# A store of one output piece, dealt in four transfers instead of one

## The chip, the cores and the metric

The kernel runs on one core of one Trainium2 chip. Its time is device microseconds from one launch to its end; the time before is the median of six runs. One execution was also taken by the hardware profiler; the profile and the trace below are of that execution.

## The reference

Cross-covariance attention over four quarters (batch entries) of 6400 rows and 256 columns, followed by a mixture of eight low-rank adapters on every row, two of the eight chosen by a gate. Only the shape of the output matters for the change: 25,600 rows of 256 fp32 numbers, 26.2 MB.

```python
qn = q / (norm(q, axis=1) + 1e-6); kn = k / (norm(k, axis=1) + 1e-6)
a = softmax(kn.T @ qn / tau)            # 256 x 256 for each quarter
x = (v @ a).reshape(25600, 256)
logits = x @ w_gate; w = softmax of the two largest of eight
out = x + sum over the chosen e of w_e * ((x @ A[e]) @ B[e])
```

## The kernel before, in words

A quarter's 6400 rows are laid on 128 partitions, 50 rows ("chunks") to a partition, so that partition p holds rows 50p to 50p+49 of the quarter. The q and k rows of a quarter come in three loads each, and its v rows in five loads of ten chunks. A piece (b, i) is quarter b, ten chunks from 10i. For each quarter the kernel accumulates k'q and the norms (`do_G`, L636), makes the softmax matrix, and then, for each of the five pieces, transposes v (`do_T`, L822), computes the gate and the adapters, and multiplies (`do_Y`, L949). `do_Ye` (L963) copies a pair of chunks of the result from PSUM into the piece's slot of the tile `Y` in SBUF (seven slots of ten chunks; `STORE`, L250), and `do_store` (L966) sends the piece to the output in HBM.

The order of the work on every engine is written out ahead of time: `make_plan` (L276) lists the steps with their costs and what they wait for, `Plan.run` (L105) plays the list through against a model of the engines, the buffers and the transfers, and the instructions are issued in the order that results. The planner sees a store as one step on SP (L434); it does not look at `SPLIT` or `SHARES`. The order of the steps, the slots and the banks are therefore the same before and after the change.

There are three places where transfers are issued. Loads go out from GpSimd (`do_load`, L613, L627; queue q0 in the profile, converting fp32 to bf16 on the way). Stores go out from SP in the order of the plan (L971; queue q1). The first q and k chunks and the weights go out from SP and ScalarE at the start. A store carries for every partition ten chunks of one piece, a run of 10,240 bytes in SBUF and in HBM, so a store of 128 partitions has 128 rows of 10,240 bytes. The last two pieces of the last quarter go in stores of 4, 4 and 2 chunks (`FINE`, L461, L432), which have shorter rows.

`HOLD` (L456) makes some stores wait for a load that has nothing to do with their data. Piece (2, 3) is in it, and waits for the load of v (0, 4), which landed long before; its wait ends at once.

The SP order from the changed store on is: (2, 3), (2, 4), (3, 0), (0, 1), (3, 1), (3, 2), three parts of (3, 3), three parts of (3, 4). Of the slots that these stores free, only that of (2, 3) is filled again, by the copies of piece (3, 4).

The lines of `do_store` that the change reaches:

```python
        for rows in SHARES if (b, i) in SPLIT else (P,):
            r = nc.sync.dma_start(out_v[b, p:p + rows, lo:lo + n, :], Y[p:p + rows, at_y:at_y + n, :])
...
            p += rows
```

Of the kernel before, what the change touches and what calls it, by code (L numbers as in the profile page):

```python
# [458 lines left out]

PARTS = {(0, 0): ((0, 4), (4, 13)), (0, 2): ((34, 8), (42, 8)), (3, 2): ((34, 8), (42, 8))}  # L460
FINE = 2  # L461
SPLIT, SHARES = set(), ()
OFF = {(0, 0, 'k'), (0, 1, 'q'), (0, 2, 'q'), (0, 3, 'q'), (0, 5, 'q'), (0, 6, 'k'), (0, 8, 'k'), (1, 0,
        'k'), (1, 1, 'k'), (1, 2, 'k'), (1, 2, 'q'), (1, 3, 'q'), (1, 4, 'k'), (1, 5, 'q'), (1, 6, 'k'), (1,
        6, 'q'), (2, 0, 'k'), (2, 0, 'q'), (2, 3, 'q'), (2, 5, 'k'), (2, 5, 'q'), (2, 6, 'k'), (2, 7, 'q'),
# [569 lines left out]
```

## Time and profile before

| what | value |
|---|---|
| median of six runs | 254.53 us (254.22 to 254.84) |
| the profiled execution: its time, its span | 254.84 us, 253.1 us |
| TensorE matmul busy | 222.7 us, 88% of the span |
| VectorE, ScalarE busy | 170.9 us (68%), 158.1 us (62%) |
| loads (q0), stores and first loads (q1) | 38.80 MB, 26.87 MB |
| instruction fetches (q8) | 19 packets, 0.31 MB |
| mean granted clock of TensorE | 0.958 |

The span runs from the first instruction to the last; the time of an execution also holds what lies around it, 1.7 us here. The profile's section 2 cuts the span in 40 slices and gives for each the busy share of every engine in tenths, the mean busy share of the 16 DMA engines, and the rate at which they moved bytes. Section 3 counts what each DMA queue moved. Section 4 is the chain of work that ended last. A DMA engine's part of a transfer is called a ring here. A transfer's landing is told to a semaphore in 16 steps; the trace keeps the time of each step, and the start, length and size of every packet that a ring moved.

### The profile page before, as it was taken

How to read it: one execution, taken by the hardware profiler on the slowest of the kernel's cores; microseconds unless marked ns; L12 is line 12 of the kernel's file. 1: busy time of each engine (PE TensorE's matmuls, PEld its weight loads, DVE VectorE, ACT ScalarE, POOL GpSimd, SP SyncE). 2: the span in 40 equal slices, each digit the busy share in tenths (PEclk: the TensorE clock that was granted, in tenths of full speed). 3: DMA queues.
4: the chain of work that ended last, by engine and by line, in shares of the span. 5: the costliest groups of instructions: out<-in, count | busy, mean ns of one | idle time of the engine just before them, and what ended most of it. 6: DMA issues, size and time to landing. Idle time of an engine off the chain costs nothing.

```text
span 253.1 us, 6005 instructions
## 1 busy us (share of the span) xinstructions
PE 222.7 (88%) x2467; PEld 197.6 (78%) x2467; DVE 170.9 (68%) x485; ACT 158.1 (62%) x294; POOL 26.6 (11%) x54
## 2 busy tenths in 40 slices
PE   0677996799999899999998998899999999999960
PEld 0465884599899898889996997699978889999940
DVE  0024374469997988786849679869996897597420
ACT  5424123276877758767665778756954948877840
POOL 7003010011000201000102203010000200000000
PEclk9959997599999999999999999999999999999996
DMA  8999999999999999999999999999999999999994
GB/s 249 216 217 210 212 221 212 214 220 214 218 211 224 308 216 221 308 292 239 220 214 302 232 217 213 210 214 215 213 312 411 418 230 322 334 403 427 422 414 180
DMA packets 11147, 66.71 MB, mean 264 GB/s; under 512 B 1264, under 2 KB 1648, under 8 KB 6512
## 3 DMA queue, kind: packets, MB, share of 16 engines
q0 software_dynamic: 6912, 38.80, 74.3%
q1 hardware_dynamic: 3872, 26.87, 25.9%
q10 hardware_dynamic: 336, 0.66, 0.8%
q8 instruction: 19, 0.31, 0.4%
q14 instruction: 8, 0.07, 0.1%
HBM read 78.91 MB, written 26.21 MB: 415 GB/s over the span
## 4 chain that ended last, share of the span: by engine, by line
PE 56%; DMA 26%; DVE 9%; ACT 4%; issue 1%; POOL 0%; POOLq 0%; DVEq 0%
PE Y_ps L955 14%; DMA qk<-in_k_dram 14%; PE acc L642 9%; PE Y_ps L960 7%; DMA v<-in_v_dram 7%; PE T_ps L828 5%; DMA out_dram<-y 5%; PE gzT_ps L942 4%; PE Z_ps L919 4%; DVE ssq L670 4%; PE ZL_ps L852 3%; PE acc L646 3%; ACT sq L664 2%; PE acc L651 2%; PE log_ps L866 2%
## 5 line engine op out<-in xcount | busy, mean ns | idle before, releaser
L642 PE MATMUL acc<-qk 128*128 128x256 bf16 x400 | 75.6, 287 | 13.2 <-ACT qk L815 6.6
L670 DVE TENSOR_TENSOR ssq<-ssq,sq 128x1280 f32<-128x1280 f32 (+1 forms) x27 | 43.3, 1604 | 25.8 <-ACT sq L664 25.5
L955 PE MATMUL Y_ps<-a_bf,vT 128*128 128x256 bf16 x400 | 60.0, 272 | 0.3 <-ACT y L810 0.3
L810 ACT COPY y<-Y_ps 128x512 f32<-128x512 f32 x83 | 47.9, 588 | 18.0 <-PE Y_ps L960 12.0
L664 ACT ACTIVATE sq<-qk 128x1280 f32<-128x1280 bf16 (+1 forms) x27 | 36.9, 1368 | 27.9 <-DMA qk<-in_k_dram 10.1
L642 PEld LDWEIGHTS <-qk 128*128 128x128 bf16 x400 | 36.1, 104 | 18.4 <-DMA qk<-in_k_dram 8.6
L955 PEld LDWEIGHTS <-vT 128*128 128x128 bf16 x400 | 38.7, 98 | 4.7 <-issue 0.5
L960 PE MATMUL Y_ps<-ball,gzT 128*128 128x256 bf16 x200 | 38.2, 273 | 0.0
L646 PE MATMUL acc<-qk 128*128 128x128 bf16 x210 | 30.2, 226 | 0.0
L651 PE MATMUL acc<-qk 128*128 128x128 bf16 x200 | 29.3, 231 | 0.0
L828 PE MATMUL T_ps<-ident,v 128*128 128x128 f32 x200 | 28.1, 274 | 0.0
L930 DVE TENSOR_TENSOR gz<-Z_ps,gateg 128x256 bf16<-128x256 f32 x60 | 22.4, 440 | 4.3 <-PE Z_ps L919 4.2
L810 ACT COPY vT<-T_ps 128x512 f32<-128x512 f32 (+1 forms) x43 | 21.7, 540 | 5.2 <-PE T_ps L828 4.9
L646 PEld LDWEIGHTS <-qk 128*128 128x128 bf16 x210 | 21.3, 101 | 3.1
L828 PEld LDWEIGHTS T_ps<-ident,v 128*128 128x128 f32 x200 | 22.1, 142 | 0.6 <-issue 0.2
L810 ACT COPY gzT<-gzT_ps 128x256 f32<-128x256 f32 (+1 forms) x45 | 14.7, 348 | 12.3 <-PE gzT_ps L942 12.2
L960 PEld LDWEIGHTS <-gzT 128*128 128x128 bf16 x200 | 19.4, 98 | 2.5 <-DVE gzT L812 0.3
L627 POOL DMA_DIRECT2D v<-in_v_dram x20 | 11.0, 551 | 98.5 <-PE T_ps L828 75.9
L651 PEld LDWEIGHTS <-qk 128*128 128x128 bf16 x200 | 19.1, 104 | 2.6
L942 PE MATMUL gzT_ps<-ident,gz 128*128 128x128 f32 x100 | 19.7, 281 | 1.4 <-DVE gz L930 1.0
L919 PE MATMUL Z_ps<-waA_sb,vT 128*128 128x128 bf16 x240 | 17.7, 219 | 0.0
L664 ACT ACTIVATE ssq<-qk 128x1536 f32<-128x1536 bf16 x8 | 11.9, 1485 | 7.1 <-DMA qk<-in_q_dram 3.6
(80 smaller groups left out, 275.4 us busy)
## 6 DMA issues: line engine op xcount, KB each, us to landing
out_dram<-y SPq DMA_DIRECT2D x18, 1280.0 KB, 12.6
v<-in_v_dram POOLq DMA_DIRECT2D x20, 640.0 KB, 25.2
qk<-in_q_dram POOLq DMA_DIRECT2D x7, 1088.0 KB, 22.6
qk<-in_k_dram POOLq DMA_DIRECT2D x7, 1088.0 KB, 27.1
qk<-in_q_dram POOLq DMA_DIRECT2D x4, 512.0 KB, 23.2
qk<-in_k_dram POOLq DMA_DIRECT2D x4, 512.0 KB, 24.8
qk<-in_q_dram POOLq DMA_DIRECT2D x2, 1024.0 KB, 30.5
qk<-in_k_dram POOLq DMA_DIRECT2D x2, 1024.0 KB, 35.0
```

What stands on the lines that cost most here:

```text
L642: nc.tensor.matmul(acc[ic][:, 0:256], kt[:, j, ic::CC], qt[:, j, :], start=c == 0, stop=False, skip_group_check=True)
L646: nc.tensor.matmul(acc[ic][:, 256:384], kt[:, j, ic::CC], kt[:, j, ic::CC], start=False, stop=False, skip_group_check=True)
L651: nc.tensor.matmul(acc[ic][:, 384:512], qt[:, j, ic * P:(ic + 1) * P], qt[:, j, ic * P:(ic + 1) * P], start=False, stop=c == NC - 1, skip_ ...
L664: nc.scalar.activation(out[:, 0:n, :], t[:, j:j + n, :], ACT.Square)
L670: nc.vector.tensor_tensor(out=t, in0=t, in1=held["sq", (w, b, g), ""][:, 0:n, :], op=OP.add)
L810: nc.scalar.copy(out, in_)
L828: nc.tensor.matmul(ps[:, j, :], vt[:, c + j, :].bitcast(FP32), W["ident32"], is_transpose=True, start=(j == 0), stop=(j == n - 1))
L919: nc.tensor.matmul(ps[:, j, :], vT_of(b, i, c + j)[:, :, ic], st[b]["aA"][:, ic, :], start=(j == 0 and ic == 0), stop=(j == n - 1 and ic = ...
L930: nc.vector.tensor_tensor(out=pairs[:, h].rearrange("p c (e r) -> p c e r", e=E), in0=z[:, 2 * h:2 * h + 2, :].rearrange("p c (e r) -> p c ...
L942: nc.tensor.matmul(ps[:, j, :], pairs[:, j * P:(j + 1) * P], W["ident32"], is_transpose=True, start=(j == 0), stop=(j == n // 2 - 1))
L955: nc.tensor.matmul(ps[:, j, :], vT_of(b, i, c + j)[:, :, ic], st[b]["a"][:, ic, :], start=(j == 0 and ic == 0), stop=False, skip_group_che ...
L960: nc.tensor.matmul(ps[:, j, :], pair[:, :, j], W["B"], start=False, stop=(j == 1), skip_group_check=True)
```

## The change

The store of piece (2, 3), the 128 rows of 10,240 bytes that are the partitions 0 to 127, goes out in four transfers of 112, 6, 6 and 4 rows (partitions 0 to 111, 112 to 117, 118 to 123 and 124 to 127), issued one after the other from SP. Only the first of them carries the `HOLD` dependency. The bytes, their source and their place in the output stay as they are.

```diff
-SPLIT, SHARES = set(), ()
+SPLIT, SHARES = {(2, 3)}, (112, 6, 6, 4)
```

## The prediction

> **What bounds the kernel now.** The change touches one store, issued at 211.61 us of a span of 253.1, so I read from the end backwards: first what ends last, then what that waits for, then whether the transfers before it have slack.
>
> The waits of SP from 244 us to the end (who waited for whom: us in total, times, longest):
>
> ```profile
> SPq L1030 <- DMA out_dram<-y: 6.4, 5, 2.8
> SPq L971 <- ACT y L810: 1.6, 2, 1.4
> ```
>
> L1030 is the end of the program. SP waits there for stores to land, five times, 6.4 us together. The compute engines are done long before: the chain of work from 244 us on ends with
>
> ```profile
> 244.32 0.59 ACT y L810
> ```
>
> (start, length), a copy that ends at 244.91, and the last store is issued at 244.93. The last step of its landing comes at 252.15 in the trace's landing records; the span ends 0.9 us later. So stores set the end. Is it their latency or their bytes? The DMA view of 226 to 253 us, in 40 slices of 0.68 us:
>
> ```profile
> DMA  9999999999999999999999999999999986631100
> GB/s 419 425 410 425 425 437 425 425 425 425 455 410 410 425 455 404 425 410 425 440 410 425 428 391 446 410 385 413 428 404 416 410 352 264 258 149 73 49 6 0
> ...
> q1 hardware_dynamic: 1664, 9.82, 87.4%
> q8 instruction: 2, 0.03, 0.4%
> ```
>
> It is bytes: the rings are 9 tenths busy or more for 32 slices, at some 425 GB/s, and then the rate falls in steps. That tail is the place of this change: some rings finish while others still work. The packets say how far apart. From 226 us each ring's packets follow one another without a gap until its last store packet, which ends at 247.6 to 248.4 us on six rings, at 249.7 to 250.3 on seven, and at 251.31, 251.34 and 251.82 on three. A store row of 10,240 bytes is one packet, and starts 381 ns after the one before it on its ring (409 on one ring of the seven). In every transfer of 128 rows each ring carries eight, so a lead or a lag once got is kept to the end. One cause of the lags is seen: an instruction fetch of 16 KB (19 of them, q8) takes 0.9 to 1.0 us of one ring, and those at 216.3 and 236.5 us hit two of the three late rings.
>
> So the end is the latest ring's: 251.82 us of packets, 0.33 to the landing step, 0.9 to close, and 1.7 around the span, 254.84 in all. That execution is 0.31 above the median of 254.53; I work in differences and put them on the median.
>
> **The change, part by part.** *SP.* Three more issues. An issue took 332 ns, up to 914 when another had just gone before, with 0.03 to 0.06 us for a wait ahead of it; three take 1.1 to 2.9 us, and SP is free at 215.2 at the latest. The next store is issued at 217.73, so this is hidden. If that cover went, the rings would still cover it: the earliest ring reaches that store's rows around 226.4. Stores take eight semaphores in turn; three more move each later store three on. One then finds its semaphore's earlier store still landing: (0, 1), issued at 224.11, would take that of the store that landed at 224.49. It goes 0.4 us late, SP has nothing behind it until 231.70, and its first rows move at about 232. Nothing.
>
> *Who waits for the store itself.* Its slot is filled again by piece (3, 4), whose first copy is this one:
>
> ```profile
> 241.22 1.24 ACT L810 COPY y<-Y_ps 128x512 f32<-128x512 f32 x2 [0.96 <-PE Y_ps L960]
> ```
>
> The store now lands at 230.59, so it may land 10 us later. The load of v (3, 4), issued at 212.35 beside it, has landed by 224.09, about when the earliest ring starts on (2, 3), and PE transposes it from 228.2. Hidden.
>
> *Fewer rows on most rings.* The 112 rows are seven a ring instead of eight. A transfer of six rows can use six rings at most. If the three small ones begin at the same ring, four rings get 7+3=10 rows, two get 9 and ten get 7: +0.76, +0.38 and -0.38 us. As all rings work without a gap to the end, that is carried to the end. If the six are early rings, they end at 249.2 or before, and the end is 251.82 - 0.38: a gain of 0.38 us. If the latest ring is one of the four, it costs 0.76. The trace does not number the rings. What it shows, as far as the landings can be followed, is that the instruction fetches go from ring to ring in turn: each later fetch makes another ring late. The rings hit longest ago are then the six early ones, neighbours in that turn. Six neighbours against six neighbours: I take it that they are the same six, as the loads' landings fall in groups of four and the fetch that follows three in the last group falls in the first.
>
> The Trainium skill, "DMA: Bandwidth & Descriptors", section "Why a DMA increments its semaphore by 16 and not by 1", says that a transfer uses the largest number of engines up to 16 that divides its rows, and on SP's queue the lowest-numbered ones: 16, 6, 6 and 4 here, all beginning at ring 0. No transfer in this trace shows fewer than 16.
>
> *Rows that change rings.* Before, ring and partitions always go together: each ring reads the same eight partitions in every store. When other rings go idle after 248 us, the packets of those left get no faster (159 ns for 4 KB before and after). So 26.9 GB/s is the limit of something private, the ring or the way into its eight partitions, and nothing here tells which. After the change, the last 16 partitions are read by six early rings, while the rings at home there are in the midst of their own rows. If the limit is the ring's, that costs nothing. If it is that of the way into the partitions, every foreign row takes its 0.38 us from the home ring, busy without a gap from 226 to 251 us. The nearest row with two streams on one path is a store row that shares its ring with a fetch: 767 ns instead of 385. The 16 foreign rows then cost a home ring 0.38 us for each that falls to it: one (spread over all 16 rings), four, or eight (if eight partitions in a row are one ring's), 0.38, 1.52 or 3.05 us. The 112 rows, dealt by sevens, also no longer match the eights: up to seven rows of a ring shared, 2.67 us more. Against it stands one row less, -0.38. So: -0.38 if nothing is shared; 0 to 5.3 if it is. Within sharing I take four foreign rows, the middle of the three, and no cost for the sevens, since rings in step could take them side by side: 1.52 - 0.38 = **+1.14 us**.
>
> A rule that speaks against the change: the Trainium skill, "SBUF — State Buffer", section "Door 1: The DMA port swizzle", has 16 ports of 27.2 GB/s with eight partitions each, and puts the partitions 112 to 127 on four of them, four rows to each. By it, four home rings lose 1.52 us each, the estimate above; without such a port the sum is -0.38. The rate of 26.9 GB/s fits, but the ring's own limit would look the same.
>
> **The rivals.**
> 1. *Shared paths* (my forecast, 0.50): +1.14 us, 255.67; up to +3.4 with part of the sevens, 257.9. For it: the 16 rows move to rings that do not hold their partitions, and those at home have no gap to spare. Against: no row shows a path being shared.
> 2. *The balance alone* (0.36): the limit is the ring's, the latest ring has one row less, -0.38, 254.15. For it: the even 381 ns, the six early rings with 3.4 us in hand. It decides if a foreign row costs the latest ring less than 0.38 us in all.
> 3. *The wrong rings* (0.07): the extra rows go to six rings among which is the latest, +0.76, 255.29.
> 4. *No effect* (0.07): the 16 rows are dealt over all 16 rings, eight each as before, 254.53.
>
> I forecast slower, though narrowly, since rival 2 needs the ring to be the only limit and rival 1 only that the path is no wider than what one ring draws from it.
>
> **How the numbers follow.** A measurement of this kernel tells about 0.2% (0.5 us) from no change. Slower by more: rivals 1 and 3, less the few cases of 1 with one foreign row on the latest ring, 0.54. Within: rival 4, most of 2 and those few, 0.39. Faster: the part of 2 in which the early ring's help is more than one row, as when late rings also gain from quieter partitions, 0.07. The range goes from rival 2 less 0.15 for the spread of a median, 254.0, to forecast and part of the sevens, 257.9. The forecast's own range is 255.0 to 257.9.
>
> **What would show it.** Store rows of 10,240 bytes at 381 ns throughout, six rings later and ten earlier by one row: rival 2. Rows at 500 to 770 ns between about 223 and 232 us, on home rings and visitors, and the DMA rate under 425 GB/s there: rival 1. The last landing moves as the latest ring does in either case. I am wrong altogether if PE or the copies end later than 244.91, or if a copy of piece (3, 4) waits for the store.

## The result, and the profile after

The changed kernel takes 255.13 us (median of 18 runs, 254.22 to 256.39) against 254.59 us (39 runs, 254.22 to 255.45): a ratio of 1.0023, 95% interval 1.0012 to 1.0035, so 0.3 to 0.9 us slower. It also spreads more: seven of its 18 runs lie above 255.5 us, and none of the kernel before. Its profiled execution lies below its median, at 254.54 us with a span of 252.8, so its span can't be set beside that of before; what happens inside it can.

The waits of SP from 244 us on and the end of the chain, in the kernel after:

```profile
SPq L1030 <- DMA out_dram<-y: 5.9, 6, 1.2
SPq L971 <- ACT y L810: 1.6, 2, 1.4
```

```profile
244.07 0.59 ACT y L810
```

The end is still SP waiting for stores. The last copy begins 0.25 us earlier in this execution than in that of before (all of it lies ahead of the changed store). The last landing step is at 252.04 us, 7.97 us after that copy began, where it was 7.83: in this pair of executions the tail is 0.14 us longer. The copy that fills the slot of piece (2, 3) again waits for PE, as before, and not for the four transfers, which have all landed by 230.61:

```profile
240.97 1.24 ACT L810 COPY y<-Y_ps 128x512 f32<-128x512 f32 x2 [0.96 <-PE Y_ps L960]
```

The DMA view of 226 to 253 us, the kernel after, again in 40 slices of 0.68 us:

```profile
DMA  9999999999999899998999899999999999752100
GB/s 334 373 394 394 410 376 440 440 425 379 425 485 425 379 425 440 464 379 349 470 485 379 364 464 440 397 388 391 419 410 398 431 394 376 316 212 106 76 0 0
...
q1 hardware_dynamic: 1682, 9.85, 89.0%
```

Two things differ from before. The tail is steeper: the rings' last landing steps lie from 248.42 to 252.04 us (247.96 to 252.15 before), and two early rings are left where there were six. And the first six slices stand at 334 to 410 GB/s, where 410 to 437 stood, at the same 9 tenths busy: the rings are occupied and move less. The same in numbers, by the windows view (stretch; its length; busy us of PE, PEld, DVE, ACT, POOL; granted clock; DMA share; GB/s); first the kernel before, then the one after:

```profile
223.00:232.00 9.00, 9.00 (x104) 8.59 (x103) 8.11 (x28) 7.22 (x17) 0.00 (x0) 1.00 1.01 425
232.00:238.00 6.00, 6.00 (x77) 5.53 (x75) 3.39 (x13) 4.32 (x10) 0.00 (x0) 1.00 1.01 424
```

```profile
223.00:232.00 9.00, 9.00 (x109) 8.57 (x108) 8.11 (x27) 6.97 (x17) 0.00 (x0) 1.00 1.00 402
232.00:238.00 6.00, 6.00 (x77) 5.52 (x73) 3.14 (x13) 4.56 (x10) 0.00 (x0) 1.00 1.00 419
```

In the 9 us in which the four transfers move, 23 GB/s are missing, 207 KB or 20 rows of 10,240 bytes: 0.48 us of each of the 16 rings. The packets show where: between 223 and 232 us rows take up to 1,044 ns, and the time that rows take beyond 385 ns adds up to 7.8 us over all rings, against 1.1 before. This is the sign that the forecast asked for, if rows that a ring reads from another ring's partitions slow somebody; the trace does not say which partitions a row is from, so the experiments have to. The question is also how the parts add up, and why to 0.5 us and not 1.1.

### The profile page after: what moved, and what is told of

It reads as the page before. It is cut to its first block, busy times and chain, and to the rows that moved or that the text cites. A ratio compares the mean times of both kernels' runs of the same rounds, so it can differ in the third digit from the quotient of the medians.

```text
span 252.8 us, 6009 instructions
## 1 busy us (share of the span) xinstructions
PE 222.3 (88%) x2467; PEld 197.5 (78%) x2467; DVE 170.9 (68%) x485; ACT 158.2 (63%) x294; POOL 26.6 (11%) x54
## 4 chain that ended last, share of the span: by engine, by line
PE 48%; DMA 36%; DVE 6%; ACT 5%; issue 1%; POOL 0%; DVEq 0%; POOLq 0%
DMA qk<-in_k_dram 25%; PE Y_ps L955 12%; PE acc L642 7%; DMA v<-in_v_dram 7%; PE Y_ps L960 6%; DMA out_dram<-y 5%; PE T_ps L828 5%; PE Z_ps L919 4%; PE gzT_ps L942 4%; PE ZL_ps L852 3%; DVE ssq L670 2%; ACT sq L664 2%; PE acc L651 2%; PE acc L646 2%; PE log_ps L866 1%
## 5 line engine op out<-in xcount | busy, mean ns | idle before, releaser
L642 PE MATMUL acc<-qk 128*128 128x256 bf16 x400 | 75.4, 286 | 13.2 <-DMA qk<-in_k_dram 6.8
```

The lines of the kernel that those rows point to most:

```text
L642: nc.tensor.matmul(acc[ic][:, 0:256], kt[:, j, ic::CC], qt[:, j, :], start=c == 0, stop=False, skip_group_check=True)
```

## The experiments

The theory is the forecast's: the way into a group of eight partitions carries no more than one ring draws, so a row read by another ring (a visit) costs its time to the ring that reads this group in a store of 128 rows (the ring at home). The rival is the balance alone: only the rings have a limit. Each kernel is timed beside runs of the kernel before on its chip. "Own" partitions are 4r to 4r+3 and 32+4r to 35+4r for ring r of the first eight, and the same 64 higher for the others.

**1. The change taken apart.** All four of the first group are one line:

```diff
-SPLIT, SHARES = set(), ()
+SPLIT, SHARES = {(2, 3)}, (112, 6, 6, 4)   # again
+SPLIT, SHARES = {(2, 3)}, (112,)           # sevens_only
+SPLIT, SHARES = {(2, 3)}, (112, 16)        # one_each
+SPLIT, SHARES = {(2, 3)}, (6, 6, 4, 112)   # small_first
```

> The change as it is, once more, beside the three others. Shared paths: the same as its first runs, 0.2 to 1.1 us above the kernel before, with store rows of 10,240 bytes at 500 to 1000 ns between 223 and 230 us and 385 ns elsewhere. Balance alone: 0.4 us below the kernel before. The rings that take the small transfers are not always the early ones: the time follows where the six landing steps of the six-row transfers lie among the sixteen of the 112-row one, -0.4 us if all six are early, up to +0.8 us if the latest ring is among the first four.

> The 112 rows alone; the last 16 partitions of piece (2, 3) are not stored, so that part of the output is left out. Every ring has one row less and no ring has a visit from the last 16. Balance alone: -0.38 us against the kernel before. Shared paths: the dealing by sevens costs something by itself, so more than -0.38, between -0.3 and +1 us; what the change lies above this kernel is the price of the 16 rows on other rings, 0.4 to 1.5 us.

> 112 rows and 16 rows: every ring still carries eight rows, but not those of its own partitions. Balance alone: no change, within 0.1 us. Shared paths: slower by 0.4 to 1.5 us, rows over 500 ns while the two transfers move. If it is as slow as the change, the balance gave nothing.

> 6, 6, 4 and then 112 rows: the same number of rows on each ring as in the change, but the rows that go to the first rings are those of the partitions 0 to 15, and the 112 are the partitions 16 to 127. Balance alone: the same as the change. Shared paths: the visits fall on the homes of partitions 0 to 15 and not of 112 to 127; if those homes are early rings the late ones are spared, 0.4 to 1.5 us below the change.

| kernel | median, before 254.52 us | ratio, 95% interval | rows beyond 385 ns, 223 to 232 us |
|---|---|---|---|
| again | 255.10 | 1.0022 (1.0008 to 1.0036) | 7.6 us |
| sevens_only | 254.69 | 1.0009 (0.9991 to 1.0027) | 4.1 us |
| one_each | 255.65 | 1.0050 (1.0026 to 1.0074) | 13.2 us |
| small_first | 255.48 | 1.0038 (1.0022 to 1.0055) | 9.4 us |

The balance alone is out: 112 and 16 rows leave every ring its eight rows, and cost 0.5%, 1.3 us. The windows view of that kernel says the same as the rows:

```profile
223.00:232.00 9.00, 9.00 (x104) 8.58 (x103) 8.11 (x28) 7.21 (x17) 0.00 (x0) 1.00 1.00 386
```

386 GB/s for 425, 0.82 us of each ring in the mean. The change is quicker than that by 0.28%, but the intervals overlap, so whether giving the 16 rows to a few rings and none to the others is worth something is not settled. The 112 rows alone, with an eighth of the store not done at all, don't come out faster: dealing by sevens (seven rows to a ring) has a price of its own.

One expectation failed: with the small transfers first, the visits fall on the partitions 0 to 15, and the kernel was to be quicker than the change; it is slower by 0.16%, within the two intervals, and surely not quicker by 0.4 us. The order also moves the 112 rows up by 16 partitions, so two things changed at once. Why it is no better stays open.

**2. The price of a visit by itself.** Three transfers of 16 rows are added to the unchanged kernel, behind the store of piece (2, 4), whose slot is not filled again. They go to a spare tensor, the same number of bytes to the same place in all three kernels, one row of every transfer on each ring; only the partitions differ.

```diff
+    spare = nc.dram_tensor("spare", (3, 16, PC, C), FP32, kind="Internal").ap()
...
             p += rows
+        if (b, i) == (2, 4):
+            for x in range(3):
+                nc.sync.dma_start(spare[x], Y[32:96:4, at_y:at_y + n, :])   # visit_own
+                nc.sync.dma_start(spare[x], Y[0:128:8, at_y:at_y + n, :])   # visit_eight
+                nc.sync.dma_start(spare[x], Y[112:128, at_y:at_y + n, :])   # visit_four
```

Each kernel has one of the three last lines. The fourth of this group splits the store of (2, 3) in two halves:

```diff
+SPLIT, SHARES = {(2, 3)}, (64, 64)         # halves
```

> Adds to the kernel before, right behind the store of piece (2, 4), three transfers of 16 rows of 10,240 bytes into a spare tensor in HBM: the partitions 32, 36, ... 92. Every ring has three rows more, 1.14 us. Shared paths, if the path belongs to the groups of eight partitions that a ring holds in a 128-row store and these groups are 0 to 3 with 32 to 35, 4 to 7 with 36 to 39 and so on: each ring reads from its own group, so 1.1 us slower and rows at 385 ns. Balance alone, no shared path: 1.1 us as well. It is the measure for the next two.

> As the last, with the partitions 0, 8, ... 120: the same rows on each ring and the same bytes, from half as many groups of partitions, two rows of each. Balance alone, no shared path: 1.1 us slower than before. Shared paths no wider than a ring: 2.3 us if the rings were in step, and between 1.5 and 3 us as they are not. A path twice as wide: near 1.1 us.

> As the last, with the partitions 112 to 127, the ones that the change sends to other rings: four groups, four rows of each in every transfer. Balance alone, no shared path: 1.1 us slower than before. Shared paths no wider than a ring: the four rings at home carry 12 rows through their path, 4.6 us, so 3 to 5 us slower, with rows of up to 1.9 us. A path twice as wide: about 2.3 us.

> The store of piece (2, 3) in two transfers of 64 rows: eight rows on every ring as before. Balance alone: no change. Shared paths: 64 partitions are on half of the groups, so two rings draw on each; in step the store would take 3.05 us longer, and 1 to 3 us slower is expected, more than for 112 and 16 rows (1.1 us).

| kernel | median, before 254.50 us | ratio, 95% interval | in us, by the ratio |
|---|---|---|---|
| visit_own | 255.38 | 1.0035 (1.0023 to 1.0047) | +0.89 |
| visit_eight | 256.40 | 1.0069 (1.0046 to 1.0093) | +1.76 |
| visit_four | 258.78 | 1.0162 (1.0130 to 1.0195) | +4.12 |
| halves | 255.98 | 1.0052 (1.0032 to 1.0072) | +1.32 |

The same number of bytes costs 0.9, 1.8 or 4.1 us by the partitions that they are read from: once, twice and between four and five times. The DMA view of 223 to 239 us (slices of 0.4 us), first visit_own, then visit_four:

```profile
GB/s 384 435 410 435 461 410 410 410 451 384 435 410 410 435 410 410 461 456 384 486 384 410 435 435 410 461 435 410 410 410 435 410 451 410 384 435 384 410 461 435
```

```profile
DMA  9999999999999999989999979279969899999999
GB/s 422 410 435 435 435 435 451 384 410 410 435 410 461 410 410 456 410 333 358 333 333 230 256 179 333 102 205 282 307 256 358 333 461 374 384 410 384 410 410 461
```

The first does not dip, and its rows take as long as in the kernel before (0.4 us in all beyond 385 ns between 228 and 232 us, as there). The second falls to 102 GB/s while nearly all rings count as busy: they wait at the same few partitions, with rows of up to 2,306 ns. That is the theory's table: 3 rows on each way are 1.14 us, 6 are 2.29, 12 are 4.57, and all three came out at 77 to 90% of that. A way twice as wide would have left visit_eight at visit_own's time.

One expectation of this group failed: halves was to be slower than one_each (112 and 16 rows), by up to 3.05 us in all if the rings were in step, and came out level with it, 1.32 and 1.27 us. Its lost rate fits its time, 57 GB/s or 1.2 us of each ring in the mean; why no more is lost stays open.

```profile
223.00:232.00 9.00, 9.00 (x104) 8.61 (x103) 8.11 (x28) 7.20 (x18) 0.00 (x0) 1.00 1.00 368
```

The Trainium skill, "SBUF — State Buffer", section "Door 1: The DMA port swizzle", has 16 ports of 27.2 GB/s, four partitions and the four 32 higher to a port; the three kernels agree with both, the grouping and the width. Its "DMA: Bandwidth & Descriptors", section "Why a DMA increments its semaphore by 16 and not by 1", has a transfer use the largest number of engines that divides its rows, the lowest-numbered ones: in the trace of the change each six-row transfer raises its semaphore once at its issue and then in six steps, and visit_own's rows at 385 ns are what ring r gives when it reads its own partitions there. That the six rings are the lowest-numbered ones no run shows by itself.

**3. The three terms, one by one, and another place.** The first kernel sends 8,960 of the 10,240 bytes of every row of (2, 3), in one transfer of 128 rows; the next two add the change's small transfers as extra work behind (2, 4), from own partitions or from the last 16; the last makes the change for another piece.

```diff
+            if (b, i) == (2, 3):                                   # seven_eighths
+                cut = n * C * 7 // 8
+                dst = dst.rearrange("p c d -> p (c d)")[:, 0:cut]
+                src = src.rearrange("p c d -> p (c d)")[:, 0:cut]
...
+        if (b, i) == (2, 4):   # six_own; six_far has 112:118, 118:124, 124:128
+            for x, part in enumerate((slice(32, 56, 4), slice(32, 56, 4), slice(32, 48, 4))):
+                m = len(range(128)[part])
+                nc.sync.dma_start(spare[x, 0:m], Y[part, at_y:at_y + n, :])
...
+SPLIT, SHARES = {(3, 2)}, (112, 6, 6, 4)                           # late_place
```

> The store of piece (2, 3) stays one transfer of 128 rows, but sends only 8,960 of each row's 10,240 bytes; the last 1,280 are left out of the output. Every ring then carries one row's bytes less, as with the 112 rows alone, and reads its own partitions. Both theories: -0.3 to -0.4 us. What the 112 rows alone lie above it is the price of dealing by sevens: 0.5 us if paths are shared, nothing if not.

> Adds to the kernel before, behind the store of piece (2, 4), transfers of 6, 6 and 4 rows into a spare tensor, from the partitions 32, 36, ... 52, again those, and 32, 36, 40, 44: the partitions that the first six rings hold themselves. The first four rings have three rows more, two have two more. If the first six rings are ahead of the latest by a microsecond or more: no change, 0 to 0.2 us. If the latest ring is among them: 0.8 to 1.1 us slower.

> As the last, but from the partitions 112 to 117, 118 to 123 and 124 to 127, as in the change: the same rings, the same rows each, other partitions. Shared paths: four homes lose four rows, 1.5 us; 0.6 to 1.5 us slower than the last kernel, since the latest ring may be at another home. No shared path: the same as the last kernel.

> The change's four transfers for piece (3, 2), the last whole store, in place of (2, 3). Shared paths: slower than before as the change is, by 0.2 to 1.1 us. Balance alone: -0.4 us.

| kernel | median, before 254.69 us | ratio, 95% interval |
|---|---|---|
| seven_eighths | 254.12 | 0.9979 (0.9967 to 0.9990) |
| six_own | 254.59 | 0.9998 (0.9989 to 1.0007) |
| six_far | 254.91 | 1.0011 (0.9999 to 1.0023) |
| late_place | 254.48 (254.15 to 256.23) | 1.0004 (0.9988 to 1.0021) |

*A row less on every ring* is worth 0.21%, 0.53 us (0.25 to 0.84; 0.38 was expected), when each ring reads its own partitions:

```profile
223.00:232.00 9.00, 9.00 (x104) 8.58 (x103) 8.11 (x28) 7.24 (x17) 0.00 (x0) 1.00 1.02 425
```

No rate is lost here (425 GB/s). *Dealing by sevens* is the difference to sevens_only, which moves the same number of bytes: 1.0009 less 0.9979, 0.30% or 0.76 us, with some 0.5 us of uncertainty from the two intervals. *The extra rows on the first six rings* cost nothing that was measured (six_own, at most 0.18 us by its interval): none of these rings is the latest, and three more transfers cost nothing by themselves. They are not the six early ones either. In six_own the first six-row transfer lands at 230.26, 230.37, 231.21, 231.86, 232.01 and 232.06 us, about one row behind rings whose store of (2, 4) landed between 229.86 and 231.67: three are early, three are of the middle group (the seven rings that ended at 250.00 to 250.65 us in before). *The visits* are six_far less six_own: 0.13%, 0.33 us, within an uncertainty of 0.4; 0.6 to 1.5 was expected. Rows took up to 1,359 ns there, and 3.1 us in all beyond 385 between 230 and 232 us.

*The later place* was expected to be slower and came out anywhere: six of twelve runs at or below 254.43 us, six between 254.54 and 256.23. Its profile (of a run of 255.42 us) shows a second thing at work. Its DMA view of 236 to 253 us, slices of 0.43 us:

```profile
DMA  9999999998999999769966999985999999961110
GB/s 386 434 400 410 458 386 458 410 458 337 458 386 386 410 313 361 289 275 337 395 275 222 424 381 405 357 337 207 400 395 419 400 405 376 405 260 58 48 39 0
```

Here the rings are not busy in places. With the four transfers and their successors queued, an issue on SP took 0.65 to 1.94 us in place of 0.33 as a rule, the last store was issued at 248.20 in place of 244.93 (0.7 of this was there ahead of the four), and the early rings ran dry; 14 of the 16 have their last landing step at 251.44 to 251.82. Of the two effects, which decides a run is not settled by one profile.

*The same terms from the traces.* From the issue of the store of (2, 3) to the last landing step, which leaves out what lies ahead of the store, before took 40.54 us in its one profiled execution. Against that, seven_eighths took -0.73 us, sevens_only -0.25, again -0.09, the change +0.14, six_own -0.01, six_far +0.14, small_first +0.44 and one_each +1.80; visit_own took +0.78, visit_eight +1.69, visit_four +4.20 and halves +1.52. By these the row less is -0.73, the sevens +0.48 and the visits +0.15 to +0.39. They are single executions, and lie up to 0.65 us off the tables: below them where a run quicker than the median was profiled (sevens_only, again, the change), above where a slower one was (one_each).

## Why the prediction was right, and where its size was off

- *What bounds the end*: right. Stores land last in every kernel here (the prediction's sum of the end, 251.82 + 0.33 + 0.9 + 1.7, is 254.75 as rounded; the last two are nearer 0.95 and 1.74, and nothing rests on it), and the compute engines' last copy moved with nothing that was done to the store. In every profile the last store is issued as much earlier or later as the store of (2, 3) was, to 0.01 us, except in late_place. What all rings gain or lose shows at the end: 0.38 us less is 0.53 less (0.25 to 0.84, seven_eighths), 1.14 more is 0.89 more (0.59 to 1.20, visit_own).
- *SP, semaphores, slot, v load*: right for the place that was chosen. The next store was issued at 217.48, the slot's copy did not wait. The store of (0, 1) waited 0.6 us for its semaphore's earlier store, to 224.06, which is 0.4 us longer than for the load that `HOLD` makes it wait for (223.65); 0.4 was worked out. Its issue itself took 1.85 us, which was not; nothing was behind it. late_place shows SP without the cover, some 2.5 us late.
- *Shared paths over the balance alone*: right, and the cause is shown: the cost goes by the partitions that are read (0.9, 1.8, 4.1 us for the same number of bytes), and 16 rows dealt over all rings cost 1.3 us without any change in the rings' shares. How the change's own half microsecond divides between the sevens and the visits is known only within the uncertainties below.
- *The size*: 0.6 us by the ratio where 1.14 was forecast. The sum had three terms. The row less was taken as -0.38 and measures -0.53. The 112 rows were taken as free, "since rings in step could take them side by side", and measure +0.76, within 0.5; the prediction's own ring ends were up to 4 us apart. The visits were taken as 1.52 and measure 0.33 in both pairs that show them (six_far less six_own, within 0.4, and again less sevens_only, within 0.6): clearly less than 1.52, but not told from nothing. -0.53 + 0.76 + 0.33 is 0.56. With again less sevens_only as the last term the sum gives again's ratio by construction; with six_far less six_own it is a check, though a wide one. Two terms were off in opposite directions, so it was luck that the sum came as near as it did.
- *A row less in the shared-path sum*: this term was worked out for the rings and added to a cost worked out for the ways into the partitions. By the theory's groups, which experiment 2 agrees with, the partitions 0 to 111 still leave twelve of the sixteen groups all their eight rows (the other four have four), and with the small transfers all sixteen have eight. A way that is the limit then has nothing less to carry, and the -0.38 need not show at all: sevens_only at 1.0009 (0.9991 to 1.0027) is what that gives. This is an argument; no run tells it from collisions of rings that are out of step.
- *Why the visits cost less than four rows*: argued, not shown. 1.52 us are taken from the four home rings, and the end moves only by what puts one of them behind the latest ring, which ended 1.5 us after the middle group (last landing steps of before: 252.15 and 250.65). The forecast counted the home rings' loss as the end's loss. visit_four does not test this: there all sixteen rings draw three rows through the same four ways, and fifteen of the sixteen last landing steps, taken in order, lie 2.7 to 4.2 us later than in before.
- *The early rings are the first six*: wrong; three or four of the six were, in three profiles. It did no harm, as the latest was not among them.
- *Open*: the spread of the changed kernel's runs, 254.2 to 256.4 us. Only runs below its median were profiled (254.54 and 254.25). That how rows collide depends on how far the rings stand apart in a run would explain it, but no run shows it. Part of every kernel's spread lies ahead of the change: the store of (2, 3) was issued between 211.22 and 212.34 us in the fourteen profiles, and the kernels are the same up to there.

## What to carry to other kernels

Which ring carries a row and which partitions it is read from are one choice: a store of 128 whole partitions lets 16 rings run side by side at 26.9 GB/s each, and every complete split of the store of (2, 3) tried here, none of them made along the rings' own partitions, cost time, up to 1.3 us for one store of 1.3 MB (one_each, halves). By the account above, taking work from a late ring by dealing its partitions to others doesn't relieve the way into these partitions, which carries the same bytes whoever asks for them. Where a loss falls on some of several parallel lanes, work out which lane ends last afterwards; only the part beyond the present last one is paid.

## What the runs showed of the hardware

- Three transfers of 16 rows took the end 0.9, 1.8 or 4.1 us back, by whether the rows lay on 16, 8 or 4 groups of partitions.
- A transfer of six rows counts once on its semaphore at its issue and then in six steps (one issued at 211.93: 212.73, then 226.62 to 229.26 us).
- An issue of a store on SP, 0.33 us as a rule, took 0.65 to 1.94 us behind the four transfers (late_place, from 237.15 us on). The issue of the store of (0, 1), 0.77 us in before, took 1.85 in the changed kernel, 2.07 in sevens_only, which has no transfer more than before, and 2.99 in one_each. What sets it is not shown.
